# Another order for a hand-written instruction list: value swaps moved between three engines, and other accumulator banks for TensorE

## The chip, the cores and the metric

The kernel runs on one core of a Trainium2 chip. A core has five engines that each work through a list of their own, in order, and wait for one another through semaphores: TensorE (PE in the profile; PEld is its loading of weights), VectorE (DVE), ScalarE (ACT), GpSimd (POOL) and SyncE (SP). SP issues data transfers and does not compute; POOL both computes and issues transfers. The metric is the device time of one execution in microseconds. Before the change the median of three runs is 193.31 us (193.24 to 193.69).

## The reference

A gated linear attention is followed by a bilinear feed-forward block:

```python
for t in range(S):                                   # B,H,S,D = 4,8,768,48
    state = alpha[:, :, t, :, None] * state + einsum('bhd,bhe->bhde', k[:, :, t], v[:, :, t])
    y[:, :, t] = einsum('bhd,bhde->bhe', q[:, :, t], state)
x = y.transpose(0, 2, 1, 3).reshape(B * S, H * D)    # 3072 x 384
out = ((x @ w_a) * (x @ w_b)) @ w_out                # 384 -> 1536 -> 384, float32
```

## The kernel before, in words

The sequence is cut into three steps of 256 positions, and the four batches into two pairs. This gives six chunks, numbered 0 to 5: chunk c is step c // 2 of batch pair c % 2. A chunk has two halves u = 0 and 1, one for each batch. Two neighbouring positions share a partition, so that 128 partitions hold 256 positions.

For a chunk the attention goes through these operations. The names are those of the list `PROGRAM`, and the letter at the end of an entry is the engine (V DVE, S ACT, P POOL, Y SP):

- `ld` loads alpha, k, q or v (line 503). `W` and `Wo` load the weights (lines 483, 486), always from POOL.
- `ln` takes the logarithm of alpha (ACT, line 510). `l2`, `l2s` add the two positions of a partition (518, 567). `H`, `L`, `R` split the sums into parts of lower precision (555, 561, 577).
- `B`, `A2`, `AQ` (545, 592, 587) make the running sums on TensorE. `dk` (654) makes the decay of a chunk on TensorE, and `dr`, `dl` (638, 643) fetch it through DRAM.
- `E` takes the exponentials, `ra` a ratio (ACT, 621, 599). `lv` and `mk`, `mq` multiply k and q by them (606, 632).
- `C` transposes q and k on TensorE (692), and `Ce` copies the result out (916 on DVE, 914 on ACT). In later chunks `T` transposes by a transfer of SP (701), and `Tr` copies the keys.
- `v` and `vs` write the values into the tile `vx`: `v` copies them (725 or 727), and `vs` swaps the two positions, for one half and one 64-row group, by two instructions of 32 partitions (914 on ACT, 916 on DVE or POOL).
- `K`, `K2` (748, 761) make the update of the state on TensorE, and `k` applies it (775, 778, 779).
- `D` (793) makes the scores. `M` masks them on the way out (DVE, 802); `Mc` copies them (ACT, 806) and `Mm` masks them later (DVE, 810).
- `SB`, `SA` (the carried state) and `Y` (the chunk itself) add up the attention's output on TensorE (822). `X` copies it out as `xT` (858 on ACT, 860 on DVE).

The feed-forward block runs on the finished chunk: `a f w i` and `b f w i` (877) multiply by column block f (0 to 11) of w_a or w_b into bank i. w is 0 or 1 for the half with 256 columns, and * for both with 512 columns. `as` copies a's result to `as_`, of which there are three buffers (ACT, 883). `pr` multiplies it with b's result, straight from the bank (DVE, 891). `o m h i` (899) adds up six of the twelve blocks for output rows m. `ot` copies the result out, `st` stores it. At the very end `oc`, `otc`, `stc` do this in half widths (910, 935).

All accumulators share eight banks of one tile, `psum`; a digit at the end of a TensorE entry names the bank. An entry that writes a bank waits until the bank's last result is read. Nothing is planned at run time: `tc.manual_schedule()` keeps the order of `PROGRAM` on each engine. An entry whose input is late holds back all entries behind it on its engine. The list interleaves a chunk's attention with the feed-forward block of the chunk before.

```python
def vswap(ch, us, g, eng):
    for x in range(2):
        to, of = (slice(g * HC + n * HQ, g * HC + (n + 1) * HQ) for n in (x, 1 - x))
        o_ = vxs[ch.c % 2][to, us, 1 - x, :, :D]
        i_ = ch.v[of, us, :, x, :]
        ...
        evict(o_, i_, eng)
```

Of the kernel before, what the change touches and what calls it, by code (L numbers as in the profile page):

```python
# [77 lines left out]
1: K2 1 1 2 3
2: ld k * P; l2s 1 V; ra 0
1: vs 1 0 S  # L80
3: ld v * P
0: cz 1 v P
1: Y 0; k 1 0 V; SA 0
0: st 3 Y
1: X 0 S; vs 1 1 V; D 1 1 6; Mc 1 1
2: R 0
1: k 1 1 V
0: o 0 0 4; o 0 1 -; c3 P
3: ld a * P
1: a 2 0 0  # L90
# [966 lines left out]
```

## Time and profile before

| | |
|---|---|
| median of three runs | 193.31 us |
| the profiled execution | 193.74 us |
| its span in the trace | 191.8 us |
| PE busy | 184.5 us |
| DVE busy | 136.8 us |
| ACT busy | 114.1 us |
| POOL busy | 52.9 us |
| moved by transfers | 29.41 MB |

The span leaves out 1.94 us of the profiled execution's time, and that execution is 0.43 us above the median. "Busy" of PE counts a matmul until its result is written, and matmuls overlap. A PE that shows almost no idle time may therefore still be waiting a little; the distance from one start to the next shows it. In a row of the timeline the columns are the start, the time to the end of the last of the instructions in it, engine, line, operation, and in brackets the idle time before and who ended it.

### The profile page before, as it was taken

The numbers are of one execution on the slowest core, as the hardware profiler recorded it, in microseconds if no ns is written. First come the engines' busy times: TensorE is split into PE (matmuls) and PEld (weight loads), VectorE is DVE, ScalarE is ACT, GpSimd is POOL, SyncE is SP. The second block draws the span as 40 slices with busy tenths as digits, with TensorE's granted clock in tenths as the row PEclk, the third lists the DMA queues.
The fourth block names the chain that finished last, engine by engine and source line by source line (L and its number), as shares of the span: only waits on it lengthen the run. The fifth ranks groups of instructions, "written<-read, shape, count | busy, mean of one in ns | idle before, by whom it ended". The sixth has DMA issues, their size and how long they took to land.

```text
span 191.8 us, 6128 instructions
## 1 busy us (share of the span) xinstructions
PE 184.5 (96%) x2597; PEld 115.2 (60%) x2613; DVE 136.8 (71%) x251; ACT 114.1 (59%) x216; POOL 52.9 (28%) x80
## 2 busy tenths in 40 slices
PE   7999999999999999999999999999999999999993
PEld 3987775666778876644446554556446555444562
DVE  2398887888998997689899996899085742234711
ACT  4446475797988888853867558775266151424321
POOL 8999506595424035000460000300030000000000
PEclk9999999999999999999999999999999999999999
DMA  5999999999994999989999988026812100210013
GB/s 137 267 221 213 254 249 239 241 265 269 252 207 86 84 205 281 257 240 156 200 296 191 180 123 201 4 82 86 177 6 82 46 3 0 82 41 3 0 68 137
DMA packets 64475, 29.41 MB, mean 153 GB/s; under 512 B 55760, under 2 KB 62816, under 8 KB 64448
## 3 DMA queue, kind: packets, MB, share of 16 engines
q1 hardware_dynamic: 46080, 16.34, 40.3%
q0 software_dynamic: 18224, 12.58, 38.0%
q8 instruction: 20, 0.33, 0.7%
q10 hardware_dynamic: 144, 0.10, 0.1%
q14 instruction: 7, 0.06, 0.1%
HBM read 25.98 MB, written 4.74 MB: 160 GB/s over the span
## 4 chain that ended last, share of the span: by engine, by line
PE 73%; DVE 12%; DMA 5%; issue 3%; ACT 3%; SPq 2%; DVEq 0%; ACTq 0%
PE psum L877 38%; PE psum L899 18%; DMA k_t<-in_k_dram 5%; PE psum L822 4%; DVE QKp L632 2%; DVE prod L891 2%; PE psum L528 2%; PE psum L692 2%; DVE vx L916 2%; PE psum L793 2%; SPq L932 1%; PE psum L748 1%; PE psum L545 1%; PE psum L910 1%; PE psum L546 1%
## 5 line engine op out<-in xcount | busy, mean ns | idle before, releaser
L877 PE MATMUL psum<-xT,wa_t 128*128 128x512 bf16 (+1 forms) x265 | 55.0, 336 | 0.6 <-DVE tmp L778 0.2
L877 PE MATMUL psum<-xT,wb_t 128*128 128x512 bf16 (+1 forms) x260 | 54.5, 335 | 0.9 <-DVE prod L891 0.3
L899 PE MATMUL psum<-wo_t,prod 128*128 128x384 bf16 x276 | 49.4, 326 | 0.0
L877 PEld LDWEIGHTS <-wa_t 128*128 128x128 bf16 x270 | 25.8, 98 | 20.6 <-issue 0.8
L877 PEld LDWEIGHTS <-wb_t 128*128 128x128 bf16 x270 | 25.5, 98 | 19.3 <-issue 0.9
L899 PEld LDWEIGHTS <-prod 128*128 128x128 bf16 x276 | 26.2, 98 | 17.6
L916 POOL COPY vx<-v_t 32x384 bf16<-32x384 bf16 x12 | 6.1, 508 | 49.8 <-ACT vx L725 40.9
L914 ACT ACTIVATE ot<-psum 128x384 f32<-128x384 f32 (+1 forms) x19 | 9.0, 472 | 11.3 <-PE psum L899 9.7
L806 ACT ACTIVATE m<-psum 128x768 bf16<-128x768 f32 x14 | 11.0, 810 | 2.9 <-PE psum L793 2.9
L606 POOL TENSOR_TENSOR q_t<-q_t,ra 128x384 f32<-128x384 f32 x4 | 4.0, 998 | 30.8 <-ACT ra L599 21.0
L916 DVE COPY ot<-psum 128x384 f32<-128x384 f32 x6 | 3.3, 557 | 11.2 <-PE psum L899 11.2
L510 ACT ACTIVATE la<-a_t 128x1536 f32<-128x1536 f32 (+2 forms) x9 | 9.5, 1054 | 2.9 <-DMA a_t<-in_alpha_dram 2.9
L858 ACT ACTIVATE xT<-psum 128x768 bf16<-128x768 f32 x10 | 7.9, 809 | 4.3 <-PE psum L822 4.3
L802 DVE TENSOR_TENSOR m<-psum,mask 128x768 bf16<-128x768 f32 x10 | 9.3, 951 | 1.3 <-PE psum L793 1.3
L632 DVE TENSOR_TENSOR QKp<-q_t,beta 128x768 bf16<-128x768 f32 x10 | 9.5, 954 | 0.6 <-DVE q_t L606 0.5
L632 DVE TENSOR_TENSOR QKp<-k_t,invb 128x768 bf16<-128x768 f32 x10 | 9.4, 953 | 0.2
L822 PE MATMUL psum<-m,vx 64*64 64x64 bf16 (+1 forms) x576 | 8.7, 205 | 0.2 <-issue 0.2
L503 POOL DMA_DIRECT2D v_t<-in_v_dram x8 | 8.5, 1063 | 0.0
L822 PEld LDWEIGHTS <-vx 64*64 64x64 bf16 x576 | 7.5, 108 | 0.6 <-issue 0.5
L725 ACT ACTIVATE vx<-v_t 128x768 bf16<-128x768 bf16 x9 | 7.6, 843 | 0.0
L822 PE MATMUL psum<-kqT,Sm 64*64 64x128 bf16 x144 | 7.6, 218 | 0.0
L914 ACT ACTIVATE vx<-v_t 32x384 bf16<-32x384 bf16 x14 | 7.3, 522 | 0.2
(278 smaller groups left out, 308.6 us busy)
## 6 DMA issues: line engine op xcount, KB each, us to landing
out_dram<-ot SPq DMA_DIRECT2D x23, 192.0 KB, 2.1
q_t<-in_q_dram SPq DMA_DIRECT2D x3, 768.0 KB, 6.2
k_t<-in_k_dram SPq DMA_DIRECT2D x3, 768.0 KB
a_t<-in_alpha_dram POOLq DMA_DIRECT2D x2, 768.0 KB, 11.3
v_t<-in_v_dram POOLq DMA_DIRECT2D x4, 384.0 KB, 11.1
a_t<-in_alpha_dram SPq DMA_DIRECT2D x2, 768.0 KB
a_t<-in_alpha_dram POOLq DMA_DIRECT2D x3, 384.0 KB, 7.8
k_t<-in_k_dram POOLq DMA_DIRECT2D x3, 384.0 KB, 6.9
```

Source lines behind the costliest of these rows:

```text
L503: eng.dma_start(out=t[:, us, hs].rearrange("p b h r d -> p (b h) (r d)"), in_=src[ch.b0 + us.start:ch.b0 + us.stop, hs, ch.s * 2 * C:(ch.s ...
L510: nc.scalar.activation(out=ch.la[:, us, hs].rearrange("p b h r d -> p (b h r d)"), in_=ch.a[:, us, hs].rearrange("p b h r d -> p (b h r d) ...
L632: eng.tensor_mul(QKp[ch.c % 2][:, u, j, :, hs, :D], src[:, u, hs].rearrange("p h r d -> p r h d"), f)
L725: nc.scalar.activation(out=o_, in_=i_, func=AF.Copy)
L802: nc.vector.tensor_mul(m, x, maskn())
L806: nc.scalar.activation(out=m, in_=x, func=AF.Copy)
L822: nc.tensor.matmul(o, lhsT=lhsT, rhs=rhs, start=(g, c) not in begun, stop=False, skip_group_check=True)
L858: nc.scalar.activation(out=o_, in_=i_, func=AF.Copy)
L877: nc.tensor.matmul(p, lhsT=(wa_t, wb_t)[w][:, kk, f * 128:(f + 1) * 128], rhs=ch.xT[:, kk, us, :], start=(kk == 0), stop=(kk == KT - 1))
L899: nc.tensor.matmul(op, lhsT=ch.prod[:, f, at:at + C], rhs=wo_t[:, f, :], start=(f == 0), stop=(f == NFF - 1))
L914: nc.scalar.activation(out=o_, in_=i_, func=AF.Copy)
L916: eng.tensor_copy(o_, i_)
```

## The change

`PROGRAM` is the only thing that differs. Every entry of the old list is in the new list once: the same loads, matmuls and copies. On POOL and SP the transfers keep nearly the order that they had. Three things differ.

1. 44 entries have another engine. Twelve swaps `vs` go to ACT, seven from DVE and five from POOL; three go from ACT to DVE. Four `v` go from ACT to DVE. `lv` exchanges four (POOL to DVE) for three (DVE to POOL). `ot` exchanges four (ACT to DVE) for three (DVE to ACT). Of `Ce`, two go to ACT and one to DVE; of `Tr`, two go each way. One `l2` goes from DVE to POOL, one `l2s` from POOL to DVE, one `X` from DVE to ACT, one `otc` from ACT to DVE. DVE has 227 entries after 226, ACT 212 after 207, POOL 56 after 62, and TensorE 323 both times.
2. Most of TensorE's feed-forward entries come in another order and use other banks.
3. POOL's `l2` of chunk 1 stands between its load issues `ld q 0` and `ld k 0` of that chunk. POOL's two `lv` of chunk 1 that stood ahead of its later issues are now with DVE.

The diff, cut to the stages that are spoken of (chunk 0, the loads of chunk 1, and the attention of chunks 3, 4 and 5):

```diff
-0: cm 0; c1; cz 0 b P; ci; ld a 0b Y; c1a; ld a 0a Y; ln 0b; cu; cz 1 b P; fill 7 0; cu2 V; cz 0 q V; cus; ld k 0b Y; ld k 0a Y; B 0b 2; ln 0a
-0: B 0a 0; ld q 0b Y; E 0b i; mk 0b V; dk 0 4; E 0b b; mq 0b V; C 0 1 5; E 0a i; mk 0a V; E 0a b; fill 2 0; ld v 0 P; ld q 0a Y; mq 0a V; de 0; Ce 0 1 V; ld a 1 P
-0: ln 1; cs 0 m P; C 0 0 1; Ce 0 0 V; ld k 1 P; K 0 0 2; k 0 0 V; ld q 1 P; cm 1; D 0 1 4; M 0 1; D 0 0 0; M 0 0; v 0 S; vs 0 1 V; SB 0 2; vs 0 0 V; B 1a 6
-0: E 1a b; mq 1a V; E 1a i; mk 1a V; B 1b 4; W b 0 256; E 1b b; mq 1b V; dk 1 0; E 1b i; de 1; C 1 0 1; cz 0 v P; Y 0; SA 0; mk 1b V; C 1 1 0; Ce 1 0 V
-0: Ce 1 1 V; D 1 0 4; ld v 1 P; K 1 0 1; K 1 1 6; X 0 S; v 1 S; Mc 1 0; D 1 1 2; Mc 1 1; W a 256 768; a 3 0 0; a 4 0 7; k 1 0 V; cz 1 q P; as 4 0; vs 1 0 V; a 5 0 1
-0: W a 0 256; a 0 0 4; as 5 0; vs 1 1 V; Mm 1 0 V; SB 1 2; W b 256 768; b 4 0 5; Mm 1 1 V; cs 1 m P; b 3 0 1; a 1 0 7
-1: ld a 0 P; ld a 1 P
-0: k 1 1 V; a 2 0 6; as 2 0; pr 4 0; K 0 1 5; k 0 1 V; SA 1; Y 1; b 2 0 6; pr 2 0; b 1 0 5; as 1 0; pr 1 0; b 5 0 7; pr 5 0; W a 768 1536; X 1 S; c2 P
-0: b 2 1 2; a 2 1 3; W b 768 1536; a 1 1 5
+0: cm 0; c1; cz 0 b P; ci; ld a 0b Y; c1a; ld a 0a Y; ln 0b; cu; cz 1 b P; fill 7 0; cu2 V; cz 0 q V; cus; ld k 0b Y; ld k 0a Y; B 0b 2; ld q 0b Y
+0: ln 0a; B 0a 0; ld v 0 P; ld q 0a Y; fill 2 4; dk 0 5; ld a 1 P; E 0b i; mk 0b V; cs 0 m P; E 0b b; mq 0b V; C 0 1 4; E 0a i; mk 0a V; E 0a b; mq 0a V; C 0 0 0
+0: Ce 0 0 V; de 0; K 0 0 5; Ce 0 1 S; D 0 1 2; ln 1; D 0 0 0; ld k 1 P; ld q 1 P; cm 1; v 0 S; vs 0 0 S; k 0 0 V; SB 0 4; B 1a 6; E 1a b; M 0 1; mq 1a V
+0: E 1a i; W b 0 256; B 1b 2; cz 0 v P; M 0 0; mk 1a V; dk 1 6; SA 0; vs 0 1 S; E 1b i; mk 1b V; Y 0; C 1 0 7; E 1b b; mq 1b V; C 1 1 0; Ce 1 0 V; ld v 1 P
+0: v 1 S; K 1 1 1; X 0 S; Ce 1 1 V; de 1; D 1 0 2; Mc 1 0; K 1 0 4; k 1 0 V; W a 256 768; a 4 0 5; as 4 0; a 3 0 0; D 1 1 6; Mc 1 1; SB 1 2; cz 1 q P; k 1 1 V
+0: vs 1 1 V; a 5 0 4; W a 0 256; a 0 0 1; Mm 1 1 V; a 2 0 5; vs 1 0 V; Mm 1 0 V; W b 256 768; b 4 0 6; b 3 0 7; as 5 0; pr 4 0; as 2 0; a 1 0 4; cs 1 m P; K 0 1 5; as 1 0
+1: ld a 0 P
+0: SA 1; Y 1; k 0 1 V; X 1 S
+1: ld a 1 P
+0: b 1 0 6; b 2 0 4; pr 2 0; W a 768 1536; c2 P; W b 768 1536
 1: ld q 0 P
-0: b 0 0 6
-1: ln 0; l2 0 V; ld k 0 P
-0: a 0 1 7
+0: b 5 0 5; pr 5 0; b 2 1 2
+1: ln 0; l2 0 P
+0: b 4 1 3; as 3 0; b 0 0 4; pr 1 0
+1: ld k 0 P
+0: as 0 0; a 2 1 5; a 0 1 6
+1: ln 1
+0: as 2 1; pr 0 0; pr 3 0
 1: ld v 0 P
-0: as 0 0; pr 0 0
-1: ld q 1 P
-0: as 3 0; a 5 1 0; b 0 1 4; as 2 1; pr 3 0; as 0 1; a 10 * 3; a 6 * 1
-1: H 0 V; L 0 V
-0: a 7 * 6; b 4 1 7; pr 2 1; a 4 1 2; pr 0 1; Wo 0 6; b 6 * 4
-1: ln 1; l2 1 V; H 1 V
-0: as 6 *; pr 6 *; b 10 * 1; as 10 *; a 8 * 3
-1: ra 0; lv 0 q P; ld k 1 P; A2 0 4
-0: as 4 1; pr 4 1; pr 10 *; a 9 * 2; a 3 1 1; Wo 6 12
+0: a 4 1 0; as 0 1; b 0 1 1; a 10 * 4
+1: H 0 V; l2 1 V; ld q 1 P; H 1 V; ra 0
+0: pr 0 1
+1: ra 1
+0: Wo 0 6
 1: L 1 V
+0: a 6 * 5; pr 2 1
+1: dk * 6
+0: a 8 * 1; as 4 1
+1: lv 0 q P; L 0 V
+0: b 10 * 0; as 10 *; pr 4 1; pr 10 *
+1: ld k 1 P
+0: as 6 *; Wo 6 12; a 1 1 7
+1: de *
 2: ld a * P
...
-1: ra 1; lv 1 q P
...
-1: lv 1 k P
...
+1: C 0 0 1; Ce 0 0 S; lv 1 q V; lv 1 k V
+2: ld k * P
...
+2: X 1 V
+3: dr; E 1 i
+2: X 0 S; a 5 * 2; a 6 * 3; as 6 *
+3: lv 1 k V; mk 1 V; lv 0 k V
+2: b 6 * 4
+3: mk 0 V
+2: a 7 * 5; as 5 *
+3: lv 0 q V; mq 0 V; vs 0 0 S
+2: pr 6 *
+4: lv 0 k V
+2: as 7 *; a 4 * 3
+3: mq 1 V; vs 0 1 S
...
+2: pr 7 *; a 0 * 6
 4: ld q * Y
...
+2: as 0 *; b 5 * 4; b 2 * 5; pr 5 *
+1: ot 0 S
+3: K2 * * 6 7; dl; k * 0 V; k * 1 V
...
+3: T 1
+4: ra 0
+2: a 2 * 6; as 9 *; pr 9 *
+1: ot 1 S
+3: Tr 0 S
+2: a 3 * 0; as 3 *; pr 3 *; b 1 * 7; as 1 *; pr 1 *; a 11 * 1; as 11 *; b 11 * 0; pr 11 *; as 2 *; pr 2 *; a 10 * 2; as 10 *; a 8 * 1; as 8 *; b 8 * 0
+3: Tr 1 V; D 0 1 2; Mc 0 1; D 0 0 4
+5: ld a * Y
+3: Mc 0 0
 1: st 2 Y
-2: Y 0; X 0 S
+4: lv 0 q P
+2: pr 8 *
+3: D 1 0 6; M 1 0
+2: b 10 * 1; pr 10 *; o 2 0 0
+4: l2 0 V
+3: SB 0 2; SB 1 4; D 1 1 6; Mc 1 1
+5: ld q * Y
+2: o 0 0 1; o 0 1 -
 4: l2s 0 V
...
-3: lv 0 q V; mq 0 V; lv 1 k V; mk 1 V; mk 0 V
-2: a 2 * 6; as 2 *
-3: T 0
-2: a 5 * 1; as 5 *; pr 5 *; a 3 * 0
-1: ot 1 S
-2: b 7 * 6; b 2 * 1; pr 2 *
-3: vs 1 0 S
-2: pr 7 *
-3: K2 * * 2 3; k * 0 V
...
-4: lv 0 q P; l2s 1 P; R 0
-3: D 0 1 0; Mc 0 1; D 0 0 4; Mc 0 0; D 1 0 6; M 1 0
-2: b 10 * 2; pr 10 *; o 0 0 3
-3: SB 0 0
...
+3: X 1 S; X 0 S
+4: lv 1 q V
+3: a 9 * 6
+4: mk 0 V; mq 0 V; T 0
+3: b 9 * 2
 4: E 1 i; mk 1 V
+3: a 6 * 3
+4: E 1 b; dr
+3: a 3 * 7
+4: mq 1 V
+5: l2 0 V; R 0
+3: b 3 * 4; as 9 *; pr 9 *
+5: R 1
+3: a 8 * 5; a 11 * 6
+2: ot 1 V
+4: T 1
+3: as 8 *
+2: st 2 Y
+4: dl
+3: b 8 * 2; b 1 * 5
+4: v 0 V
+3: as 6 *; as 3 *; a 1 * 0
+5: ra 0; lv 0 q P
+3: pr 8 *; b 6 * 7; pr 6 *; pr 3 *
+1: st 1 Y
+3: as 1 *; pr 1 *; a 2 * 2
+2: ot 0 S
+3: as 11 *; b 11 * 3; pr 11 *; b 2 * 0; as 2 *
+5: lv 0 k V; AQ 6; ld v * P; E 0 b; E 1 b
+2: st 1 Y
+5: E 0 i
+4: K * 0 1
+3: a 0 * 2; a 4 * 3; pr 2 *; a 5 * 0; b 0 * 6
+4: Tr 1 V
+3: as 0 *
+4: Tr 0 V
+3: as 4 *; as 5 *
+4: k * 0 V
+2: o 3 0 2
+4: D 1 1 0
+5: E 1 i
+4: Mc 1 1
+3: pr 0 *
+4: v 1 V; vs 0 1 S; D 0 1 4
+5: lv 1 k V
+4: D 0 0 6; M 0 0; M 0 1
+2: o 3 1 -; ot 3 S; st 3 Y
+3: b 4 * 0; pr 4 *; b 5 * 1; pr 5 *
+4: vs 1 1 S; SB 1 2; D 1 0 4; Mc 1 0; SB 0 6
+5: dr; mk 0 V
+3: a 7 * 0; as 7 *; b 7 * 1; o 2 0 4; b 10 * 0; a 10 * 5
+4: SA 0; SA 1; vs 0 0 S
+3: as 10 *
+5: mq 0 V; T 0
+4: vs 1 0 V; Mm 1 0 V; Mm 1 1 V; Y 1; X 1 S; Y 0
+5: mk 1 V
+3: o 3 0 5; pr 7 *
 5: ra 1
-4: E 1 b
-2: ot 1 S
-3: a 2 * 2; as 2 *; a 6 * 5; as 6 *
-5: l2s 0 V; R 0; R 1
-4: dr; mq 1 V; T 1
...
-5: vs 0 1 P
-3: ot 1 V
-5: SB 0 2; D 0 1 6; Mc 0 0
-3: st 3 Y
-5: M 0 1; SB 1 0
-4: b 7 * 4; pr 7 *; b 1 * 5; pr 1 *; b 11 * 6; b 10 * 7; a 5 * 4; as 5 *
-5: Mm 1 1 V
...
+5: SB 0 0; vs 0 1 S
+3: st 3 Y; ot 1 S
+5: D 0 1 4; M 0 1; SB 1 6
+4: b 10 * 3; pr 10 *; a 5 * 2; b 5 * 4; b 1 * 3; as 5 *
+5: vs 0 0 S; Mm 0 0 V
```

More of the change, by code (lines that the diff above doesn't have):

```diff
@@ L77 @@
-0: o 2 1 -
[L78 to L90, printed above, removed]
+0: a 7 * 3; as 8 *; pr 8 *; as 3 1; b 3 1 1; pr 3 1; b 9 * 2
+1: E 1 i; v 0 S
+0: as 9 *; pr 9 *; b 7 * 6; b 1 1 0; as 7 *; pr 7 *; a 11 * 5; as 11 *; as 1 1; pr 1 1
+1: C 0 0 1; Ce 0 0 S; lv 1 q V; lv 1 k V
+2: ld k * P
+0: a 5 1 2; b 5 1 3; as 5 1; pr 5 1; o 2 0 5
@@ L91 @@
+1: C 0 1 0; vs 0 1 S; K2 0 0 1 2
+3: ld v * P
+1: D 0 0 6; vs 0 0 S
+0: pr 11 *
+1: Mc 0 0
+0: cz 1 v P; o 1 0 3; o 3 0 4; o 3 1 -; ot 3 S
+1: Ce 0 1 V; D 0 1 6
+0: c3 P
+1: k 0 0 V; k 0 1 V; mk 1 V; mq 1 V
+0: st 3 Y
+3: ld a * P
+1: SB 0 0; M 0 1; Mm 0 0 V; v 1 V
+2: ln *; l2s 1 V; l2 0 V
+0: o 0 0 2; cs 1 0 P
+1: C 1 0 4
+2: l2s 0 V; R 0
+1: Ce 1 0 S
+0: o 1 1 -; ot 1 S
+1: C 1 1 6; Ce 1 1 S
+0: o 2 1 -
+1: K2 1 1 3 4; k 1 0 V
+2: lv 1 k P
+1: SA 0; vs 1 0 S; Y 0; k 1 1 V
 2: R 1
-0: ot 0 S; st 0 Y
@@ L328 @@
[L328 to L343 removed]
+2: K2 * * 1 7; dl; k * 0 V
@@ new lines @@
+1: b 11 1 3; b 9 1 4; a 11 1 5; as 9 1; pr 9 1; a 0 1 2; as 1 1; pr 1 1; o 2 0 0; a 3 1 1
+2: k * 1 V; vs 1 1 S
+3: l2s 0 V
+1: as 11 1; pr 11 1; a 8 1 4
+2: Tr 1 S
+1: as 0 1
+2: T 0
+1: b 0 1 5; pr 0 1; b 3 1 2
+4: ld a * Y
+1: as 3 1; pr 3 1; a 4 1 1; as 4 1; as 8 1; b 8 1 6; a 7 1 7; as 7 1; o 2 1 -
+3: l2s 1 P
+2: D 1 0 2; D 1 1 4
+3: v 0 V
+1: pr 8 1
+3: ld q * Y
+2: v 0 S; Tr 0 V; D 0 0 6
+1: ot 2 V
+2: M 1 1
+1: o 0 0 1; b 4 1 0
+2: Mc 0 0
+3: R 0; ld k * Y
+1: b 7 1 4; pr 7 1; pr 4 1
+2: Mc 1 0; vs 0 0 S
@@ new lines @@
+1: o 0 1 -
+2: SB 1 2; Mm 0 0 V; SB 0 4; vs 0 1 S; Mm 1 0 V; D 0 1 6; Mc 0 1
+3: R 1
+1: o 3 0 0; o 3 1 -; ot 3 S
+3: AQ 6
+2: SA 1
+4: ld k * Y
+3: E 1 b; E 0 b
+2: Mm 0 1 V; Y 0
+3: v 1 V; lv 1 q V
+1: st 3 Y
+3: E 0 i
+0: st 2 Y
+2: vs 1 0 V; Y 1
+3: ra 0
+2: SA 0
+1: o 1 0 0; o 1 1 -
+3: vs 1 0 V
+2: X 1 V
[9 more added lines that the diff above has]
+2: as 7 *; a 4 * 3
@@ new lines @@
+5: ld a * Y
+3: Mc 0 0
+1: st 2 Y
+4: lv 0 q P
[6 more added lines that the diff above has]
+2: o 0 0 1; o 0 1 -
+4: l2s 0 V
+2: o 2 1 -
+4: l2s 1 P
+5: ln *
+4: R 0; R 1; AQ 6
+3: Mm 1 1 V; vs 1 1 P; Y 1; SA 0; Mm 0 0 V; Mm 0 1 V; SA 1
+5: l2s 0 V; l2s 1 V
+2: ot 2 S
+4: E 0 b
+3: Y 0
+5: ld k * Y
+2: o 1 0 0; o 1 1 -
+4: E 0 i; lv 1 k P
+1: st 0 Y
+4: ld v * P
+3: X 1 S; X 0 S
+4: lv 1 q V
+3: a 9 * 6
+4: mk 0 V; mq 0 V; T 0
@@ new lines @@
+5: ra 1
+3: pr 10 *; o 3 1 -
+5: v 1 V; lv 1 q V; mq 1 V
+4: X 0 S; b 3 * 0; a 4 * 1
+5: vs 1 0 S
+4: as 4 *; a 8 * 2
+2: st 0 Y
+4: b 8 * 3; as 8 *; pr 8 *; b 4 * 1; pr 4 *; a 9 * 2
+5: T 1
+3: ot 3 S
+4: a 3 * 3; as 9 *; as 3 *; b 9 * 1; pr 9 *; pr 3 *; a 0 * 5
+3: o 0 0 2
+4: as 0 *; b 0 * 3; pr 0 *
+3: o 0 1 -; ot 0 V
+5: Tr 1 S
+4: a 7 * 5; as 7 *
+3: o 2 1 -
+5: Tr 0 V; D 0 0 0; K * 0 5; D 1 1 2
+3: ot 2 V
+5: dl; k * 0 V; Mc 0 0; D 1 0 6
+4: b 6 * 4; a 6 * 0; as 6 *; a 2 * 5
+5: Mc 1 1; M 1 0
```

310 lines of the change are left out of this document (67 added, 243 removed).

## The prediction

> **What bounds the kernel.** I read the page's shares first, then the chain that ended last, then TensorE's timeline, and for each of its holes the timeline of the engine named.
>
> ```profile
> span 191.8 us, 6128 instructions
> PE 184.5 (96%) x2597; PEld 115.2 (60%) x2613; DVE 136.8 (71%) x251; ACT 114.1 (59%) x216; POOL 52.9 (28%) x80
> DMA  5999999999994999989999988026812100210013
> PE 73%; DVE 12%; DMA 5%; issue 3%; ACT 3%; SPq 2%; DVEq 0%; ACTq 0%
> ```
>
> TensorE is busy for 96% of the span, and its matmul count stays. Only its waits can be saved, and no engine has to be faster for that. "Busy" overstates it, since matmuls overlap; the chain gives their true spacing:
>
> ```profile
> 56.65 8.62 PE psum L877 x78
> 108.02 4.91 PE psum L877 x22
> 178.89 4.88 PE psum L899 x30
> ```
>
> A matmul of 256 columns costs 8.62 / 78 = 0.11 us, one of 512 columns 0.22, one of `o` 0.163. An `a` or `b` of half width is then 0.33 us, of full width 0.65, an `o` 0.98. With these I looked for starts that come too late. The first group lies in chunk 0 (TensorE's timeline):
>
> ```profile
> 22.06 0.49 PE L877 MATMUL psum<-xT,wa_t 128*128 128x256 bf16 x3 [0.17 <-DVE tmp L778]
> 22.80 0.49 PE L748 MATMUL psum<-v_t,QKp 64*64 64x48 bf16 x16 [0.26 <-DVE prod L891]
> 23.92 1.48 PE L877 MATMUL psum<-xT,wb_t 128*128 128x256 bf16 x12
> ```
>
> `a 2` and `K` waited for DVE to read banks, and `Y 1` stood behind them; the `b` after it starts at 23.92. Four later holes follow:
>
> ```profile
> 85.39 1.46 PE L877 MATMUL psum<-xT,wb_t 128*128 128x512 bf16 x6
> 87.28 0.70 PE L761 MATMUL psum<-v_t,QKp 64*64 64x48 bf16 x64 [0.42 <-DVE QKp L632]
> 98.79 0.81 PE L877 MATMUL psum<-xT,wb_t 128*128 128x512 bf16 x2 [0.27 <-DVE prod L891]
> 104.46 0.51 PE L822 MATMUL psum<-m,vx 64*64 64x128 bf16 x28 [0.18 <-issue]
> 150.11 0.59 PE L877 MATMUL psum<-xT,wb_t 128*128 128x512 bf16 x2 [0.16 <-issue]
> ```
>
> The brackets add up to 1.03 us. The distance of the starts says more: six matmuls from 85.39 need 1.3, yet `K2` starts 1.89 later, which is 0.17 above its bracket. With 0.1 more at each, as part of the 0.17 is a change of matmul form that stays, the four are worth 1.4 us.
>
> Behind them stands DVE:
>
> ```profile
> 79.13 0.96 DVE L860 CAST xT<-psum 128x768 bf16<-128x768 f32 x1 [1.54 <-PE psum L822]
> 117.19 0.73 DVE L891 TENSOR_TENSOR prod<-as__2475,psum 128x512 bf16<-128x512 bf16 x1 [0.97 <-PE psum L877]
> 80.00:100.00 20.00, 19.15 (x196) 9.42 (x197) 18.46 (x30) 12.16 (x23) 5.29 (x6) 1.00 1.02 228
> 100.00:120.00 20.00, 19.72 (x296) 10.93 (x297) 17.88 (x31) 13.59 (x25) 0.00 (x0) 1.00 1.22 175
> ```
>
> The last two are stretches of 20 us; behind their length come PE, PEld, DVE, ACT and POOL. DVE works 18.46 and 17.88 of 20 us, ACT 12.16 and 13.59.
>
> **The change part by part.** Prices are means by form:
>
> ```profile
> L632 DVE TENSOR_TENSOR QKp<-q_t,beta 128x768 bf16<-128x768 f32 x10 | 9.5, 954 | 0.6 <-DVE q_t L606 0.5
> L802 DVE TENSOR_TENSOR m<-psum,mask 128x768 bf16<-128x768 f32 x10 | 9.3, 951 | 1.3 <-PE psum L793 1.3
> L810 DVE TENSOR_TENSOR m<-m,mask 128x768 bf16<-128x768 bf16 x14 | 7.2, 547 | 0.2
> L916 DVE COPY vx<-v_t 32x384 bf16<-32x384 bf16 x22 | 6.6, 298 | 0.4
> L577 DVE TENSOR_TENSOR lh<-l 128x768 f32<-128x768 f32 x4 | 3.8, 949 | 0.1
> L916 DVE COPY kqT<-psum 128x1024 bf16<-128x1024 bf16 x5 | 3.4, 687 | 0.7 <-PE psum L692 0.6
> L606 DVE TENSOR_TENSOR k_t<-k_t,a_t 128x384 f32<-128x384 f32 x6 | 3.3, 551 | 0.2 <-DMA k_t<-in_k_dram 0.2
> L632 DVE TENSOR_TENSOR QKp<-k_t,prod 128x384 bf16<-128x384 f32 x4 | 2.3, 584 | 3.7 <-ACT prod L621 3.5
> L778 DVE TENSOR_TENSOR tmp<-psum,Sm 128x192 f32<-128x192 f32 x4 | 1.4, 353 | 0.6 <-PE psum L748 0.6
> L891 DVE TENSOR_TENSOR prod<-as__1997,psum 128x512 bf16<-128x512 bf16 x1 | 0.7, 730 | 0.0
> ...
> L914 ACT ACTIVATE vx<-v_t 32x384 bf16<-32x384 bf16 x14 | 7.3, 522 | 0.2
> ...
> L916 POOL COPY vx<-v_t 32x384 bf16<-32x384 bf16 x12 | 6.1, 508 | 49.8 <-ACT vx L725 40.9
> ```
>
> A swap (two instructions) costs 0.60 us on DVE, 1.04 on ACT, 1.02 on POOL. Twelve more on ACT and three fewer are +9.4 us there, which 114.1 of 191.8 can carry; DVE loses four net, 2.4 us. Neither number is the gain: what counts is who is late.
>
> (1) *Chunk 0.* In the new list `vs 0 0` stands on ACT ahead of the exponentials of half 1a, and `vs 0 1` ahead of those of 1b. ACT had these gaps there:
>
> ```profile
> 13.63 0.87 ACT L621 ACTIVATE prod<-psum 128x384 f32<-128x384 f32 x2 [1.55 <-PE psum L546]
> 17.36 0.81 ACT L858 ACTIVATE xT<-psum 128x768 bf16<-128x768 f32 x1 [1.23 <-PE psum L822]
> ```
>
> The first swap of 1.04 fits into the 1.55, so the first exponential still starts at 13.63 and ends about 14.1. From there DVE is the path: `mq`, `M`, `mk`, `mk`, `mq` (4 x 0.58 + 0.95), two `Ce` (1.37), `k` of half 1 (about 3 x 0.35), `vs`, `Mm`, `vs`, `Mm` (2 x 0.60 + 2 x 0.55) make 8.0 us. Neighbours overlap by roughly 0.08 a row (the `prod` rows of 0.73 follow each other every 0.61 to 0.65), so 8.0 is an upper end and the lower end is about 7.0. I have no reason to leave the middle and add 0.4 for the two waits inside (`C 1 1` to `Ce`, `Mc` to `Mm`). `Y 1` then starts at 14.1 + 7.5 + 0.4 = 22.0, and the next `b` 0.7 later at 22.7 to 22.8 instead of 23.92. TensorE has nine halves (2.9 us), the scores and the carried state to do meanwhile, with banks that ACT frees instead of DVE. **-1.1 us**, between -1.6 and 0 (if ACT is late).
>
> (2) *Loads of chunk 1.* `l2` on POOL waits for the logarithm behind `X 1`, near 24.5, and takes about 1.0; so `ld k 0` is issued at about 25.6 instead of 18.55, and v, q, and the output weights behind it as much later.
>
> ```profile
> 18.55 0.89 POOL L503 DMA_DIRECT2D k_t<-in_k_dram  x1
> 30.46 1.00 POOL L606 TENSOR_TENSOR q_t<-q_t,ra 128x384 f32<-128x384 f32 x1 [7.73 <-DMA q_t<-in_q_dram]
> ```
>
> What hides it is the backlog: `q_t`, ahead of k in the same queue, landed only at 30.46, and the transfers were at nine tenths or more in slices 2 to 12. If k takes the 5 us left until then for its way, the queue never runs empty: 0. Without that cover it would cost the 7 us less the work TensorE has in stock, some 2 us. The two `lv` that leave POOL free its issue of k and v for chunk 2; hidden too.
>
> (3) *Chunk 1*, 44 to 57 us: ACT gets `vs 1 0` ahead of `X 0`, 1.04 us, while DVE gets room. Small waits go and come; 0, between -0.4 and +0.5.
>
> (4) *Chunks 3 and 5.* `K2` of chunk 3 needs both `mk`. In the new list DVE does `X 1`, two `lv`, two `mk` first (0.95 + 1.1 + 1.9 = 4.0 us after `Y`), before any `mq`, while TensorE has `SA`, two `o` and nine full entries ahead of `K2` (2.1 + 5.8). That is 4 us of reserve, so the hole at 87.28 goes even if k lands 2 us later. After the scores `b 10` takes bank 1, freed by ACT's `as 8` and no longer by a `prod`: the hole at 98.79 goes. At 104.46 the masks now come before both `Y`; at 150.11 `SB 1` and `b 10` meet banks long read. **-1.4 us**, between -1.7 and -0.5.
>
> (5) *The price, chunk 4.* From `l2s` of chunk 5 to `pr 10` of chunk 3 DVE has 40 instructions in the new list: 12 `pr` 8.8, 7 `mk`/`mq` 6.7, 2 `R` and 2 `M` 3.8, the other 17 about 8.4; 27.7 us by means, 24.5 with an overlap of 0.08 each. I take 26. TensorE has 24 full entries (15.6), seven `o` (6.9) and small work (about 4) against it: 26.5. So the two run level. Bank reuse has reserves of 0 to 0.3 us there (`b 8` after `pr 9`, `a 1` after `ot 1`, `a 7` and `b 7` after `pr 4` and `pr 5`, `Y 1` after `Mm`); five such places at 0.16 make **+0.8 us**, between 0 and +3.
>
> (6) Thin reserves elsewhere: the key copy `Tr 0` of chunk 2 behind its transfer, `b 10` of chunk 0 against the landing of its weights: **+0.4**, 0 to +1.
>
> Sum: -1.1 + 0 + 0 - 1.4 + 0.8 + 0.4 = -1.3 us on the profiled execution (193.74, its span of 191.8 and 1.94 around it): 192.4. That execution was 0.43 above the median, so the median goes from 193.31 to **192.0 us**. The end (one `otc` from ACT to DVE) stays.
>
> The Trainium skill's page "Perfetto Trace Analysis", section "Optimizing Scalar/DVE Operations", says that moving work from DVE to ScalarE may make sense if DVE is saturated. In chunk 0 it is not, so that by this rule the swaps there should have stayed. I go by the two gaps of ACT quoted under (1); what the rule would mean here is the second rival.
>
> **The rivals.**
>
> *DVE sets the pace in chunk 4 (slower).* Under (5) DVE has 26 us of work against TensorE's 26.5. Every wait of DVE beyond 0.5 us there, for an exponential behind `X 1` and `X 0` on ACT or for chunk 5's logarithm, is TensorE's too. The gain is used up at 0.5 + 0.8 + 1.3 = 2.6 us of idle time; at 4.5 us the median is 193.31 - 1.3 + 2.2 = 194.2. For it: the two engines run level. Against it: the old list has the same pressure (18.46 and 17.88 of 20), and DVE was hardly idle between 79.13 and 117.19.
>
> *The swaps make ACT late in chunk 0.* If the second swap holds up the exponentials of 1b by its 1.04 us, (1) shrinks to -0.1 and the median is 193.0. By the skill's rule it is this case. Against it: 1.55 and 1.23 us of idle ACT.
>
> *Nearly all holes go.* Without (5) and (6): 193.31 - 1.1 - 1.4 = 190.8.
>
> **How the numbers follow.** The forecast of 192.0 (191.3 to 192.7) gets 0.46, nearly all holes gone 0.14, ACT late 0.16, DVE's pace 0.24. A measurement here can tell 0.3%, or 0.58 us, from no change: 192.73 to 193.89. ACT late is "same" for the most part (0.12 of 0.16), DVE's pace mostly "slower" (0.23 of 0.24). So faster 0.64, same 0.13, slower 0.23. The range of 190.7 to 194.3 takes in the ends of (1), (4) and (5) and leaves some 0.2 out.
>
> **What would show it.** TensorE's first `b` after chunk 0's `Y 1` at 22.7; POOL's `k_t` issue near 25.6 with no gap in the transfers; `K2` of chunk 3 without a wait for QKp; new short waits for `prod` and `ot` some 10 to 25 us after it; ACT busy about 120 us. The prediction is wrong if DVE stands idle for over 2 us in chunk 4's preparation, or if the late loads leave the queue empty near 29 us.

## The result: 0.5% faster, by other steps than the forecast's

| | before | after |
|---|---|---|
| median | 193.56 us (18 runs) | 192.48 us (18 runs) |
| the profiled execution | 193.74 us | 192.09 us |
| its span | 191.8 us | 190.3 us |

The ratio is 0.9948 (95% interval 0.9926 to 0.9969), a gain of 0.52%; the forecast was 0.68%. The span lost 1.5 us. The page of the changed kernel, its lines for span, busy time, transfers and chain:

```profile
span 190.3 us, 6117 instructions
PE 183.6 (96%) x2598; PEld 114.4 (60%) x2613; DVE 134.0 (70%) x248; ACT 122.8 (65%) x230; POOL 46.9 (25%) x69
DMA  5999999999999589999999299726703100102014
PE 86%; POOL 6%; DMA 5%; issue 1%; ACT 0%; POOLq 0%; ACTq 0%
```

ACT rose from 114.1 to 122.8 us (forecast about 120), DVE fell by 2.8. DVE's 12% of the chain that ended last are gone: PE has 86% where it had 73, and POOL has 6%. The 5% of transfers are now one load of w_b in chunk 0, which the forecast did not have; before, they were the load of k for chunk 3. What TensorE still waits for, in the view of waits (time in all, times, longest):

```profile
PE psum L512 <- DVE og L412: 1.2, 1, 1.2
PE psum L861 <- DMA wb_t<-in_moe_w_b_dram: 0.7, 1, 0.7
PE psum L529 <- ACT la L494: 0.3, 1, 0.3
PE psum L676 <- DVE QKp L616: 0.3, 1, 0.3
PE psum L777 <- DVE kqT L900: 0.2, 1, 0.2
PE psum L861 <- issue: 0.2, 1, 0.2
```

The wait for QKp before `K2` is no longer among them (L676 is a transpose in chunk 0), and none for a `prod` is left. The one for w_b is new. (Line numbers are 16 lower than before.)

TensorE does the same work in both, so its timeline can be cut at entries that both lists have. Three marks do: `AQ` of chunk 2, `D 1 0` of chunk 3, and the last `oc`. The lengths are differences of the starts of these entries:

| us | start to AQ | AQ to D 1 0 | D 1 0 to last oc |
|---|---|---|---|
| before | 54.04 | 44.12 | 89.85 |
| after | 53.99 | 43.52 | 89.11 |
| after_again (below) | 53.57 | 43.34 | 89.10 |

The gain lies in the second and third stretch, 0.6 and 0.74 us; the first 54 us, where the forecast put 1.1, gave nothing in this trace. More entries have the same work of TensorE ahead of them in both lists, and their starts say where the gain came:

| us | before | after |
|---|---|---|
| start to `B 1a` of chunk 0 | 12.03 | 12.33 |
| on to `AQ` of chunk 2 | 42.01 | 41.66 |
| on to `AQ` of chunk 3 | 23.41 | 23.16 |
| on to `D 1 1` of chunk 4 | 45.06 | 43.97 |
| on to the last `oc` | 65.50 | 65.50 |

The first two rows differ by no more than one list differs from itself: in old_to_98 (below) the old list needs 11.32 and 41.68 us there. The 23.41 comes again in that trace, and the 23.16, to 0.01 us, in the nine other traces that have the new list's order there. So about 1.1 us came from chunk 3, 0.25 from chunk 2, and nothing that can be told from the spread from chunks 0, 1 and 5.

TensorE's timeline of the changed kernel at the places of the forecast:

```profile
22.05 0.83 PE L861 MATMUL psum<-xT,wb_t 128*128 128x256 bf16 x6 [0.71 <-DMA wb_t<-in_moe_w_b_dram]
24.20 2.03 PE L861 MATMUL psum<-xT,wb_t 128*128 128x256 bf16 x17
...
85.69 1.46 PE L861 MATMUL psum<-xT,wb_t 128*128 128x512 bf16 x6
87.17 0.69 PE L745 MATMUL psum<-v_t,QKp 64*64 64x48 bf16 x64
...
149.36 0.59 PE L861 MATMUL psum<-xT,wb_t 128*128 128x512 bf16 x2 [0.16 <-issue]
```

The first `b` behind `Y 1` of chunk 0 starts at 24.20, not at 22.7; `b 4`, ahead of it, sat 0.71 us waiting for its weights. `K2` of chunk 3 starts without a wait. The hole in chunk 5 is still there.

### The profile page after: what moved, and what is told of

It is laid out like the page before. It is cut to its first block, busy times and chain, and to the rows that moved or that the text cites. A ratio compares the mean times of both kernels' runs of the same rounds, so it can differ in the third digit from the quotient of the medians.

```text
span 190.3 us, 6117 instructions
## 1 busy us (share of the span) xinstructions
PE 183.6 (96%) x2598; PEld 114.4 (60%) x2613; DVE 134.0 (70%) x248; ACT 122.8 (65%) x230; POOL 46.9 (25%) x69
## 4 chain that ended last, share of the span: by engine, by line
PE 86%; POOL 6%; DMA 5%; issue 1%; ACT 0%; POOLq 0%; ACTq 0%
PE psum L861 49%; PE psum L883 24%; PE psum L806 5%; DMA wb_t<-in_moe_w_b_dram 5%; PE psum L777 2%; PE psum L571 1%; PE psum L745 1%; PE psum L894 1%; POOL v_t L487 1%; PE psum L676 1%; POOL wa_t L467 1%; POOL mask L443 1%; PE psum L732 1%; POOL q_t L487 0%; POOL a_t L487 0%
## 5 line engine op out<-in xcount | busy, mean ns | idle before, releaser
L861 PEld LDWEIGHTS <-wa_t 128*128 128x128 bf16 x270 | 25.6, 98 | 19.7 <-issue 0.5
L898 ACT ACTIVATE ot<-psum 128x384 f32<-128x384 f32 (+1 forms) x17 | 8.2, 479 | 17.3 <-PE psum L883 16.2
L898 ACT ACTIVATE vx<-v_t 32x384 bf16<-32x384 bf16 x32 | 16.7, 521 | 0.6
L900 DVE COPY ot<-psum 128x384 f32<-128x384 f32 (+1 forms) x8 | 4.2, 530 | 8.2 <-PE psum L883 6.1
L842 ACT ACTIVATE xT<-psum 128x768 bf16<-128x768 f32 x11 | 8.7, 811 | 1.2 <-PE psum L806 1.2
L794 DVE TENSOR_TENSOR m<-m,mask 128x768 bf16<-128x768 bf16 x14 | 7.4, 554 | 0.4 <-ACT m L790 0.3
L605 ACT ACTIVATE beta<-psum 128x384 f32<-128x384 f32 x10 | 4.7, 492 | 3.0 <-PE psum L576 2.2
```

The source lines that it names most:

```text
L605: nc.scalar.activation(out=o_, in_=i_, func=AF.Exp, scale=sc)
L794: eng.tensor_mul(m, m, maskn())
L842: nc.scalar.activation(out=o_, in_=i_, func=AF.Copy)
L861: nc.tensor.matmul(p, lhsT=(wa_t, wb_t)[w][:, kk, f * 128:(f + 1) * 128], rhs=ch.xT[:, kk, us, :], start=(kk == 0), stop=(kk == KT - 1))
L898: nc.scalar.activation(out=o_, in_=i_, func=AF.Copy)
```

## The experiments

Executions of one kernel spread by 1 to 4 us, more than the parts at stake. The second and third stretch between the marks came out within 0.2 us of each other in two traces of the changed kernel, so most readings go by the stretches; the ratio to the kernel before, with its interval, stands beside.

### after_again: what repeats

No edit.

> The changed kernel once more, unaltered, to see what of its first 25 us repeats. In its first trace the second piece of w_b (issued at 12.92) landed on fifteen transfer engines by 20.9 and on the last at 22.0, and TensorE waited 0.7 for it. If the late landing belongs to the new list, it is at 21.8 to 22.2 again and the first b after Y 1 of chunk 0 stands at 24.2; if it was this one execution, the landing is near 21 and that b near 23.4 to 23.9.

Ratio 0.9948 (0.9922 to 0.9973), span 189.7. The wait for w_b came again, 0.71 us, and with it the delay of `Y 1`: that `b` starts at 23.77, 0.81 behind the start of `SA 1` and `Y 1` at 22.96, as in the first trace (24.20 behind 23.39). The landing is at 21.58. The 0.43 us between the two traces arose in the first 12 us.

The wait does not come each time, though. Four traces further below have the same list and the same order of loads up to here, and in none of them does `b 4` wait: it starts at 21.00 in c3_mk_late, 20.65 in c4_dve_plus, 20.59 in l2_back and 20.61 in new_to_79, and the piece of w_b landed there between 20.38 and 20.87. Yet the four reach `AQ` of chunk 2 hardly earlier (53.23 to 53.57). In c4_dve_plus later loads take the time back:

```profile
20.65 0.82 PE L862 MATMUL psum<-xT,wb_t 128*128 128x256 bf16 x6
22.91 2.14 PE L862 MATMUL psum<-xT,wb_t 128*128 128x256 bf16 x18
26.47 1.47 PE L862 MATMUL psum<-xT,wa_t 128*128 128x512 bf16 x6
29.74 0.82 PE L862 MATMUL psum<-xT,wb_t 128*128 128x512 bf16 x3 [0.23 <-DMA wb_t<-in_moe_w_b_dram]
```

The `b` behind `Y 1` starts at 22.91, near the forecast. Then `a 10` and `b 10` start right behind the landings of the third pieces of w_a (26.42) and w_b (29.69), and `AQ` of chunk 2 comes at 53.39, only 0.18 earlier than in after_again.

### Order without engines, and engines without order

Each of the 44 entries got the engine of the other list; nothing else changed. Four of them, in the direction of the first kernel:

```diff
-0: vs 0 0 S
+0: vs 0 0 V
-2: vs 0 0 S
+2: vs 0 0 P
-2: Tr 0 V
+2: Tr 0 S
-4: X 1 S
+4: X 1 V
```

> The new order of the list, with the engines of the old list in all 44 entries. My theory: the order carries the gain (the masks of chunk 3 ahead of the key product, the banks of the scores read by ScalarE long before they are written again), so TensorE's K2 of chunk 3 again starts without a wait, and the kernel is 0.4 to 1.2 us faster than the kernel before. The rival, that the moved swaps carry it, expects no gain (within 0.3 us of the kernel before).

> The old order of the list, with the engines of the new list in all 44 entries. My theory: no gain, between 0 and 1.5 us slower than the kernel before, because the holes at 87.28, 98.79 and 103.9 come from the order and stay, and the swaps now stand in front of other work on ScalarE. The rival, that the moved swaps carry the gain, expects 0.5 to 1.0 us faster.

Both theories fell. The new order alone gives 207.32 us, ratio 1.0763 (1.0725 to 1.0802); the new engines alone 206.76, ratio 1.0721 (1.0694 to 1.0747). TensorE's waits in the first (three lines) and in the second (two lines):

```profile
PE psum L778 <- ACT kp L899: 1.7, 1, 1.7
PE psum L807 <- ACT vx L899: 1.7, 1, 1.7
PE psum L746 <- DVE kqT L901: 1.7, 1, 1.7
```

```profile
PE psum L823 <- ACT vx L915: 1.8, 2, 1.5
PE psum L878 <- ACT as__1496 L884: 1.1, 1, 1.1
```

In the first, the key copy `Tr 0` of chunk 2, again with ACT, stands behind two value copies there, and the scores wait 1.7 us for it. There are some ten such places in each kernel, in all stages: the three stretches are 61.62, 47.33 and 92.88 us in the first kernel, 57.34, 47.75 and 96.00 in the second. (In the first, an estimated 2.7 us are not waits: from 13 to 19 us TensorE's clock was at 0.50, and half of the 5.54 us that it was busy there is 2.77.) Neither half of the change carries the gain; an entry's place in the list is right only for the engine it was placed with.

### c0_wb_first: the weights that chunk 0 waits for

```diff
-0: E 1a i; W b 0 256; B 1b 2; ...
+0: E 1a i; B 1b 2; ...
-0: Mm 1 0 V; W b 256 768; b 4 0 6; ...
+0: Mm 1 0 V; W b 256 768; W b 0 256; b 4 0 6; ...
```

> The changed kernel with one load issue of POOL moved: the first piece of w_b, needed only after Y 1, is issued behind the second piece, which b 4 and b 3 need. My theory: the landing of the second piece is the last releaser in chunk 0, so b 4 starts near 21.2 instead of 22.05 and the first b after Y 1 at 23.4 instead of 24.2: 0.5 to 0.8 us faster than the changed kernel. The rival, that the chain of ScalarE and DVE (the second Mm ended at 22.65) would have held Y 1 anyway, expects at most 0.2 us and that b at 23.9 or later.

Ratio 0.9941 (0.9916 to 0.9967), span 189.5. In chunk 0 `b 4` starts at 20.60 without a wait, and the `b` behind `Y 1` at 22.84, where my theory had 23.4. The stretch up to `AQ` fell from 53.57 (after_again) to 52.68. That the moved load did this is not shown: l2_back and c4_dve_plus, with the order of loads of the changed kernel, have that `b 4` at 20.59 and 20.65. The last stretch rose from 89.10 to 89.81, and of the 0.5 to 0.8 us expected of the whole kernel the ratio shows no more than 0.13 (0.9941 against 0.9948). The rows of TensorE in chunk 0, and of DVE and TensorE in chunk 4:

```profile
20.60 0.82 PE L861 MATMUL psum<-xT,wb_t 128*128 128x256 bf16 x6
22.84 2.14 PE L861 MATMUL psum<-xT,wb_t 128*128 128x256 bf16 x18
...
119.44 0.56 DVE L763 TENSOR_TENSOR Sm<-tmp,bl 128x384 bf16<-128x384 f32 x1 [1.62 <-DMA bl<-row]
120.68 0.37 PE L777 MATMUL psum<-kqT,kp 64*64 64x128 bf16 x16 [0.52 <-DVE prod L875]
```

DVE waited 1.62 us for the decay that comes through DRAM, a product behind it was late, and TensorE's scores with it. Of the 0.9 us that this trace was ahead of after_again, 0.7 were given back 97 us later.

### wb_dl: the decay of chunk 4 fetched earlier

On top of c0_wb_first:

```diff
 4: T 1
+4: dl
 3: as 8 *
 2: st 2 Y
-4: dl
```

> The changed kernel with the load order of c0_wb_first, and in chunk 4 the fetch of the decay (dl) issued by SP ahead of the store st 2 instead of behind it. In c0_wb_first VectorE waited 1.62 us for that fetch (page: bl from row), and TensorE's D 0 1 of chunk 4 came 0.67 late behind it. If SP's order is the cause, the fetch lands about 1 us earlier, D 0 1 waits no more than 0.1, and the span falls from 189.5 to about 188.9. If the transfer itself is what is slow (the two transposes ahead of it in the queue), the wait stays over 1 us and the time does not move.

The last stretch is 89.10 again, and DVE does not wait for the decay. But SP's order is not shown to be the cause, and the trace of c0_both (next) speaks against it. SP has the old order there and issues the second part of the fetch at 113.88, in c0_wb_first at 113.94, yet DVE does not wait:

```profile
118.44 0.56 DVE L763 TENSOR_TENSOR Sm<-tmp,bl 128x384 bf16<-128x384 f32 x1
```

The transfer itself differs, as the rival had it: the fetch lands at 116.72 in c0_both and at 119.31 in c0_wb_first, and the packets of 4 bytes in the 7 us behind the first issue, nearly all of them the fetch's, take 0.0095 us in the mean in c0_both and 0.0151 in c0_wb_first. In the trace of wb_dl they take 0.009, so that it did not meet the slow transfer, and what the earlier issue is worth against it stays open. With `dl` in its old place, c0_wb_first, c4_dve_plus, old_to_98 and c3_mk_late have a wait of 0.88 us or more for this fetch; after, after_again, c0_both and l2_back have none. What makes the transfer slow is open.

The traced execution itself is long (span 192.2) because TensorE's clock was halved in chunk 0, which the edit does not touch; in the other eleven executions of this kernel the mean clock was 0.997 or more. The ratio, 0.9941 (0.9919 to 0.9963), shows no gain over c0_wb_first.

### c0_both: the swaps of chunk 0 back on DVE

On top of c0_wb_first:

```diff
-0: v 0 S; vs 0 0 S; k 0 0 V; SB 0 4; B 1a 6; E 1a b; M 0 1; mq 1a V
+0: v 0 S; k 0 0 V; SB 0 4; B 1a 6; E 1a b; M 0 1; vs 0 1 V; vs 0 0 V; mq 1a V
-0: SA 0; vs 0 1 S; E 1b i; mk 1b V; ...
+0: SA 0; E 1b i; mk 1b V; ...
```

> The changed kernel with the load order of c0_wb_first, and the two swaps of chunk 0, half 0, back from ScalarE to VectorE, right behind M 0 1, where VectorE stood idle for 2.58 us. In c0_wb_first the exponentials of half 1 ran at 13.56 and 15.53 behind those swaps, while their sums were ready near 13.2 and 14.5. The rival of the prediction (the swaps make ScalarE late; the rule of the Trainium skill, page Perfetto Trace Analysis, section Optimizing Scalar/DVE Operations) expects the exponentials near 13.2 and 14.6, the second Mm 0.4 earlier, and the first b after Y 1 at 22.4 instead of 22.84. My step (1), in which the swaps fit into ScalarE's gaps, expects that b within 0.15 of 22.84.

Ratio 0.9936 (0.9911 to 0.9961), span 189.6. ACT's rows of the changed kernel, then of this one, and TensorE's next wait in this one:

```profile
13.04 1.06 ACT L898 ACTIVATE vx<-v_t 32x384 bf16<-32x384 bf16 x2
14.12 0.87 ACT L605 ACTIVATE prod<-psum 128x384 f32<-128x384 f32 x2
16.10 0.87 ACT L605 ACTIVATE prod<-psum 128x384 f32<-128x384 f32 x2
```

```profile
13.18 0.87 ACT L605 ACTIVATE prod<-psum 128x384 f32<-128x384 f32 x2 [0.92 <-PE psum L530]
14.48 0.87 ACT L605 ACTIVATE prod<-psum 128x384 f32<-128x384 f32 x2 [0.43 <-PE psum L530]
22.67 2.14 PE L861 MATMUL psum<-xT,wb_t 128*128 128x256 bf16 x18
26.77 1.47 PE L861 MATMUL psum<-xT,wa_t 128*128 128x512 bf16 x6 [0.65 <-DMA wa_t<-in_moe_w_a_dram]
```

Without the swaps ACT does the two pairs of exponentials at 13.18 and 14.48, each as soon as its sums are ready; in c0_wb_first they were at 13.56 and 15.53. So the second rival was right that the swaps make ACT late, and my step (1), in which they fit into ACT's gaps, was wrong: in c0_wb_first the second pair started 0.90 us after its sums ended (14.63), here 0.04 after (14.44). Less of it reaches DVE's end. The second `Mm` ends at 21.67 instead of 22.08, 0.41 earlier, but 0.19 of this is there before the swaps, as `B 1a` starts at 11.57 instead of 11.77. The `b` starts only 0.17 earlier, and counted from `B 1a` not at all (11.10 us against 11.07), because `b 4` waits 0.18 for w_b; and at 26.77 TensorE waits 0.65 for the next piece of w_a. The stretch up to `AQ` is 53.29, longer than 52.68.

### best: all of it, and the next load cut in two

On top of c0_both, `dl` as in wb_dl, and in the feed-forward block of chunk 0:

```diff
-0: ... W a 768 1536; c2 P; W b 768 1536
+0: ... W a 768 1152; W a 1152 1536; c2 P; W b 768 1536
-0: ... a 10 * 4
+0: ... a 6 * 4
-0: a 6 * 5; ...
+0: a 10 * 5; ...
-0: b 10 * 0; as 10 *; pr 4 1; pr 10 *
+0: b 6 * 0; as 6 *; pr 4 1; pr 6 *
```

> The changed kernel with four things: the load order of c0_wb_first, the two swaps of chunk 0 half 0 on VectorE (c0_both), dl of chunk 4 ahead of st 2 (wb_dl), and the load of w_a columns 768 to 1536 cut in two, with blocks 6 and 10 exchanged in the list, so that TensorE first needs only the half that comes first (c0_both waited 0.65 us for that load at 26.77). My theory, that transfers are the last releaser of chunk 0 in turn and these are all of them: no wait of TensorE for a transfer over 0.3 us after 20 us, span 188.5 to 189.0, 0.8 to 1.2 us faster than the changed kernel. The rival, that each removed wait is given back by the next thing that is late, expects the span of c0_wb_first and c0_both, 189.5, again.

191.40 us (6 runs), ratio 0.992 (0.9894 to 0.9946): the fastest of the study, though the interval overlaps that of the changed kernel. Span 189.5: the rival's number, and my theory fell. The wait for w_a is gone, and TensorE's timeline shows the next one:

```profile
29.38 0.82 PE L861 MATMUL psum<-xT,wb_t 128*128 128x512 bf16 x3 [0.47 <-DMA wb_t<-in_moe_w_b_dram]
```

Up to 30 us each wait removed was, in these traces, answered by the load behind it. The transfers run at nine tenths or more through that time, and no load order moves fewer bytes.

### c3_mk_late: the keys' products back behind the queries'

```diff
-3: lv 1 k V; mk 1 V; lv 0 k V
+3: lv 1 k V; mk 1 V; lv 0 q V
-3: mk 0 V
+3: mq 0 V
-3: lv 0 q V; mq 0 V; vs 0 0 S
+3: vs 0 0 S; mq 1 V
...
 2: pr 7 *; a 0 * 6
+3: lv 0 k V; mk 0 V
```

> The changed kernel with lv 0 k and mk 0 of chunk 3 behind mq 0, mq 1 and the products 6 and 7 on VectorE, as late as in the old list; the rest unchanged. In the changed kernel mk 0 ended at 83.5 and K2 started at 87.17 without a wait. Step (4): mk 0 then ends at 88.1, K2 waits 0.8 to 0.9 us for it, and the kernel loses 0.7 to 1.0 us. The rival, that the hole of K2 was hidden work of TensorE and its end came from elsewhere (fewer changes of matmul form): under 0.3 us.

Ratio 0.9946 (0.9925 to 0.9968), no difference that the medians can show. The trace shows it: up to `AQ` (53.57) and behind `D 1 0` (89.11) this kernel and after_again are alike to 0.01 us, and between them it needs 43.84 instead of 43.34. DVE's and TensorE's rows:

```profile
86.23 0.96 DVE L617 TENSOR_TENSOR QKp<-k_t,invb 128x768 bf16<-128x768 f32 x1
87.25 0.70 PE L746 MATMUL psum<-v_t,QKp 64*64 64x48 bf16 x64 [0.54 <-DVE QKp L617]
```

`K2` waits for the last `mk` and the end comes 0.51 us later (186.52 against 186.01). So step (4) has its cause right, and the loss of 0.5 lies between the two expectations: `mk 0` ended at 87.2 and not at 88.1.

### c4_dve_plus: how much room DVE has in chunk 4

```diff
-4: mq 1 V
+4: mq 1 V; xv 2
```

`xv 2` is two additions on a tile that nothing else uses.

> The changed kernel with two additions of 128 x 384 f32 on a scratch tile (0.55 us each, 1.1 in all) on VectorE in chunk 4's preparation, between mq 1 of chunk 4 and l2 0 of chunk 5; the output is not touched. Step (5) has VectorE and TensorE level there, with 0 to 0.5 us to spare: 0.6 to 1.1 us slower than the changed kernel, with a new wait of TensorE for a prod near 112. If VectorE has more room there than step (5) said (it did not make TensorE wait in the changed kernel), 0 to 0.3 us.

192.82 us, ratio 0.9982 (0.9960 to 1.0003), against 0.9948 without it: 0.34% or 0.65 us slower, with intervals that overlap. The last stretch is 90.56 us, 1.46 longer. TensorE's waits, and the additions:

```profile
108.41 1.14 DVE L942 TENSOR_TENSOR scr<-scr 128x384 f32<-128x384 f32 x2
111.78 1.46 PE L862 MATMUL psum<-xT,wb_t 128*128 128x512 bf16 x6 [0.66 <-DVE prod L876]
114.74 0.81 PE L862 MATMUL psum<-xT,wa_t 128*128 128x512 bf16 x3 [0.20 <-DVE prod L876]
120.94 0.56 DVE L764 TENSOR_TENSOR Sm<-tmp,bl 128x384 bf16<-128x384 f32 x1 [1.54 <-DMA bl<-row]
```

In the trace all of the 1.1 us came through: TensorE needs 13.47 us from `Y 0` of chunk 3 to `K` of chunk 4 instead of 12.29, and another 0.27 behind the decay, whose fetch was slow here. DVE has no room there, as step (5) said.

### l2_back: the first `l2` of chunk 1 back on DVE

```diff
-1: ln 0; l2 0 P
+1: ln 0; l2 0 V
```

> The changed kernel with l2 of chunk 1, half 0, back from POOL to VectorE, so that POOL issues k of chunk 1 near 18.5 instead of 26.9. Step (2): the queue is full until then, so k lands at 31.8 instead of 32.7 and the time stays within 0.3 us of the changed kernel. The rival, that the late issues cost time (the share of transfers in 28 to 30 us was 0.82 where the kernel before had 1.15): 0.5 to 1.0 us faster.

193.34 us, ratio 1.0001 (0.9969 to 1.0033): not faster, so the rival fell. Against the changed kernel (0.9948) it is 0.5% or 1 us slower, more than the 0.3 that step (2) allows, though the two intervals just meet. Here `k` of chunk 1 is issued at 18.40 and lands at 32.4, in the changed kernel at 26.91 and lands at 32.7 (the trace's landing records): 8.5 us of issue time are worth 0.3 of landing. TensorE's timeline shows two waits that the changed kernel has not:

```profile
25.75 0.82 PE L861 MATMUL psum<-xT,wa_t 128*128 128x256 bf16 x6 [0.21 <-DVE prod L875]
78.37 0.72 PE L806 MATMUL psum<-m,vx 64*64 64x128 bf16 x48 [0.45 <-DVE vx L900]
```

The first stands behind the `l2` now on DVE. The second follows a wait of DVE for `q` of chunk 3; whether it belongs to the edit is open.

### old_to_98 and new_to_79: halves of the two lists joined

Old list, with its engines and banks, up to `pr 10` of chunk 2, new list for the rest; and new up to `SA 0` of chunk 2, old for the rest. No diff says more.

> Old order and engines up to pr 10 of chunk 2 (about 98 us), new order and engines for all that is left: the new list's part from chunk 3's scores on, alone. By step (5) of the prediction the new chunk 4 costs 0.8 us and the hole at 104.46 gives back 0.3: 0.5 us slower than before. By the traces (no new wait in chunk 4, the hole before Y gone) it is 0.3 to 0.5 us faster than before.

> New order and engines up to SA 0 of chunk 2 (about 79 us), old order and engines for all that is left: the new list's chunks 0 to 2 alone. By the prediction chunk 0 gives 1.1 us and the rest costs 0.4: 0.7 faster. By the traces chunk 0 gives nothing and chunks 1 and 2 together 0.5: 0.3 to 0.6 faster, with the hole of 0.4 at K2 of chunk 3 back.

old_to_98: 193.38 us, ratio 1.0026 (1.0000 to 1.0052). Its last stretch is 90.44 us, longer than the old list's (89.85) and than the new list's behind its own first part (89.11). DVE waits 1.28 us there for the decay of chunk 4, and TensorE 0.4 us for a `prod` ahead of chunk 3's `SB 0`; neither whole list has the second. The first is the slow fetch told under wb_dl, and it takes 0.37 us (65.87 instead of 65.50 from `D 1 1` on). My reading from the traces fell; the forecast's number (0.5 slower) came out, but for this mixture alone and with the help of that fetch.

new_to_79: 198.12 us, ratio 1.0258 (1.0227 to 1.0289), by a wait of 4.2 us at the joint (`X 0` of chunk 2 behind other work of ACT), behind which TensorE's clock was at 0.50 from 81 to 87 us. It says nothing of the parts, with one exception: its last stretch, the old order, needs 89.13 us. It seems that with the other engines some microseconds ahead, as they can get during that wait, the old order has no holes there either.

## Why the forecast was right, and where it was not

The median came out at -0.52% where -0.68% was forecast, and the sum of the steps at -1.4 us (last `oc` at 186.62 instead of 188.01) where -1.3 stood. That the number came out is luck: two large terms were wrong and cancelled, and the second trace of the changed kernel, with its last `oc` at 186.01, gives -2.0. What was right is the holes of chunk 3.

(1) *Chunk 0, -1.1 forecast, 0 measured.* This is the step that failed: it took DVE's chain for the only path. The chain itself was sized well: from `mq` at 14.65 to the end of the second `Mm` at 22.65 are 8.0 us, with the waits in it, where 7.5 and 0.4 stood. Two things were left out. The first is ACT: the sums of half 1 end at 13.90 and 15.20, and the exponentials start at 14.12 and 16.10, behind the two swaps. The second is the loads. The new list reaches `b 4` near 21.2, behind `a 2` at 20.84, and waits until 22.05 for the second piece of w_b, issued at 12.92; the old list reached it without a wait, since its load had landed at 20.16:

```profile
20.73 0.83 PE L877 MATMUL psum<-xT,wb_t 128*128 128x256 bf16 x6
```

This wait came in two of six traces of the new list. In c4_dve_plus, where it did not come, the `b` behind `Y 1` stood at 22.91, near the forecast of 22.7 to 22.8, and the third pieces of w_a and w_b took most of it back before `AQ`. So up to 30 us TensorE follows the loads in these traces, and chunk 0 had no 1.1 us to give. Step (6) did look at one of these loads, at `b 10` and with +0.4, but did not take it as a limit on step (1).

The rule of the Trainium skill, page "Perfetto Trace Analysis", section "Optimizing Scalar/DVE Operations", that DVE's work may go to ScalarE if DVE is saturated, was read in the prediction as speaking against these two swaps, since DVE was not saturated in chunk 0. For the old list that reading was wrong: from 8 to 16 us of its trace DVE is busy for 7.67 of 8 us. For the new list it is right: from 12 to 14 us DVE is busy for 0.37 of 2 us, and there c0_both agrees with the rule. Back on DVE, the swaps bring the second `Mm` about 0.2 us nearer to `B 1a`. The price forecast for that rival, 1.04 us, is near what the second pair of exponentials lost (0.86, as 0.90 less 0.04); DVE had `M 0 0` to do meanwhile, so little of it reached its end.

(2) *Late loads of chunk 1, 0 forecast.* Right about the landing, as l2_back shows, where the 1 us in the medians stays open. The issue came at 26.91 instead of 25.6. The share of transfers fell to 0.82 of an engine's time between 28 and 30 us, and nothing waited.

(3) *Chunk 1, 0 forecast, 0 measured.* The new list gains 0.29 us on the first trace between `SB 1` and `b 1` of chunk 1, but the old list in old_to_98 gains the same.

(4) *Chunks 3 and 5, -1.4 forecast, -1.1 measured* (45.06 to 43.97 in the table of the result). The holes at 87.28, 98.79 and 104.46 went; c3_mk_late shows the cause of the first, and that of the other two is read from the list and was not tried. The fourth, at 150.11, stayed, 0.16 us by its row in both kernels: that row names "issue" as what ended the wait, not an engine. I had taken it for a bank that is read late. The brackets of the other three rows named DVE twice and "issue" once.

(5) *Chunk 4, +0.8 forecast, 0 measured.* The balance was right, as c4_dve_plus shows: 1.1 us more on DVE costs 1.2. The bank reserves were there as well, but none fell below zero, so five places at 0.16 were a price for nothing. The stretch of 89.10 us comes up in five kernels of this study, so that it is probably TensorE's own time. In c0_wb_first, c4_dve_plus and old_to_98 a late decay lengthened it, by a slow transfer that the step did not have. In the changed kernel DVE was idle for 2.4 of 24 us (21.62 busy between 88 and 112), which the forecast had named as a sign of failure. The sign came without the failure: no wait of TensorE for a `prod` followed.

(6) *Elsewhere, +0.4 forecast:* chunk 2 gained 0.25 instead (23.41 to 23.16); what made it was not tried. The load at `b 10` belongs to (1).
